# Seven row blocks normalised on GpSimd, none on ScalarE, in a newly ordered attention-plus-gated-MLP kernel on one Trainium2 core

## The chip, the cores and the metric

The kernel runs on one core of one Trainium2 chip. The core has five instruction queues that run on their own and wait for each other through semaphores: TensorE (PE, matrix multiplies), VectorE (DVE), ScalarE (ACT), GpSimd (POOL) and SyncE (SP), which here issues nearly all DMAs. The metric is the device time of one execution in microseconds (us): the median of three runs before the change is 272.52 us (272.19 to 273.63).

## The reference

One pre-norm transformer layer over 2048 rows of width 640 in bf16, with a linear attention of 32 heads of 20 and a gated MLP of width 1536:

```python
def _A_ref(x, wqkv, w_phi, wo):
    ...
    pq = jnp.einsum("bhsd,hdf->bhsf", q, w_phi)
    pk = jnp.einsum("bhsd,hdf->bhsf", k, w_phi)
    phi_q = jnp.concatenate([_softmax(pq, axis=-1), _softmax(-pq, axis=-1)], axis=-1)
    phi_k = jnp.concatenate([_softmax(pk, axis=-1), _softmax(-pk, axis=-1)], axis=-1)
    kv = jnp.einsum("bhsf,bhsd->bhfd", phi_k, v)
    z  = jnp.einsum("bhsf->bhf", phi_k)
    ...
    o = num / den
    return (lambda x, *d: x.transpose(*d))(o, 0, 2, 1, 3).reshape(B, S, D) @ wo
def _B_ref(x, w_gate, w_up, w_down):
    g = jnp.einsum("bsd,df->bsf", x, w_gate)
    u = jnp.einsum("bsd,df->bsf", x, w_up)
    h = g * u
    return jnp.einsum("bsf,fd->bsd", h, w_down)
h = x + _A_ref(_layernorm(x, axis=-1), A_wqkv, A_w_phi, A_wo)
h2 = h + _B_ref(_layernorm(h, axis=-1), B_w_gate, B_w_up, B_w_down)
```

## The kernel before

The 2048 rows are 16 tiles of 128 (t = 0 to 15). Each piece of work is an *operation* with a name, made by `G.op`; its engine, emitter, inputs and outputs stand beside the name. The names that the text uses, with the tile's number behind them:

- `x`: load of one or two x tiles. `w5`: load of the feature weights, 25 KB. `wk`, `wv`: 128 rows of the K and V weights. `wqt`: transposing load of a piece of the Q weights. `wo`, `wg`, `wu`, `wd`: the later weights.
- `L1s`, `L1a`: the row statistics of the first norm on VectorE (lines 406 to 409). `L1l`, `L1e`: logarithm and exponential on ScalarE, which give one over the standard deviation in `rs` (L414, L417).
- `L1n`: a 128x1 operation that puts minus mean times `rs` into `nb` (L421), the *shift* of the ScalarE form below.
- `xn`: the normalised tile. VectorE computes (x minus mean) times `rs` (L431); ScalarE computes x times `rs` plus `nb` (L429). In the kernel before, 13 tiles are made on VectorE and three (7, 10 and 11) on ScalarE.
- `xt`: the transposed tile in `xnT`; tiles 0 and 1 by TensorE (`xte` takes the result out of PSUM), all others by a DMA transpose that SP issues (L449).
- `WT`, `WTe`: transposes of the K weights on TensorE, and their evacuation. `Ph0` to `Ph2`: the block-diagonal feature weights, which need `w5` (L358). `F1`, `F0`: the feature weights folded into the K and the Q weights on TensorE (L389), with evacuations `Fe`. F1 needs all `Ph` and a `WTe`, F0 needs all five `wqt`.
- `K`, `V`, `Q`: projections of a tile on TensorE, ten matmuls each (L460). `Kx`: two exponentials on ScalarE (L472); `Ks`: the sums on VectorE (L476); `Kr`, `Ke`: their reciprocal on ScalarE (L479, L481); `Kn`: the division, 128x1280 on GpSimd (L496). `KV`: kv and z, accumulated on TensorE over all 16 tiles (L504); `KVe` takes them out after KV15.
- `Qx`, `Qs`, `Qr`, `Qb`, `Qe`, `Qn`: the same for Q (L529 to L548, `Qb` and `Qn` on GpSimd); `qT`: DMA transpose of the result (L553). `N`: numerator and denominator (L566); `dd`, `rd`, `o`: the division; `oT`: its DMA transpose (L597); `O`: output projection (L603); `h`, `hc`, `hT`: residual, centring, DMA transpose.
- `U`: gate and up projections (L646) in five blocks of rows, `D`: down projection (L665), `y` and `w`: the last addition and the store.

Where an operation stands is written out by hand in a table of text, `PLAN`: name, place, the number of an alternative engine (0 or left out is the first), and the PSUM banks or buffers that it takes. `arrange` sorts by place and hands each engine its operations; every engine then works strictly in that order, and SP issues its DMAs strictly in that order. An operation at the head of a queue that waits holds up all that stand behind it. The few lines that decide this:

```python
k, a, o.slots = PLAN.get(name, (key, 0, ()))
o.eng, o.occ, o.lat = o.alts[a]
...
for o in sorted(G.ops, key=lambda o: (o.key, o.i)):
    order[o.eng].append(o)
```

Of the kernel before, what the change touches and what calls it, by code (L numbers as in the profile page):

```python
# [57 lines left out]
F1_0:75::4 xn1:76::3 F1_2:77::0 L1e3:78 Fe1_0:79:1 WTe3:80 L1n3:81 WT4:82::2 xt1:83::3 xn3:84::0 Fe1_2:85:1 F1_3:86::6 xte1:87:1 K0_0:88::4 xt3:89 Fe1_3:90
K0_1:91 WTe4:92:1 K0_2:93 L1s2:94 V0_0:95::0 F1_4:96::2 wqt0:97 V1_0:98::6 Fe1_4:99:1 V1_1:100 L1s4:101 K0_3:102 V1_2:103 K1_0:104::2 L1a2:105 L1s5:106
wqt3:107 L1l2:108 K1_1:109 K0_4:110 L1e2:111 K1_2:112 L1n2:113:1 L1a4:114 K1_3:115 L1a5:116 xn2:117::2 L1l4:118 K1_4:119 V0_1:120 L1e4:121 Kx0_0:122::0  # L60
xt2:123 V0_2:124 L1n5:125:1 L1n4:126 xn5:127::3 V0_3:128 Kx0_1:129 V0_4:130 L1s6:131 V1_3:132 Kx1_0:133::1 V1_4:134 x10:135 V3:136::4 L1s7:137 Kx1_1:138
xt5:139 Ve1:140::0 L1a6:141 xn4:142::0 K3:143::2 Ks0:144::0 Ve3:145::1 x8:146 Ve0:147::2 xt4:148 K2:149::4 L1a7:150 Ks1:151::1 L1l6:152 Kx3_0:153::2 wqt4:154
Kx3_1:155 V2:156::0 L1s11:157 L1e6:158 Kx2_0:159::3 L1n6:160 wqt1:161 L1n7:162 Kr0:163 Ks3:164::2 Kx2_1:165 K5:166::2 Ke0:167 Kr1:168 wqt2:169 Ve2:170::3
Kn0:171 xn6:172::3 V5:173::4 xn7:174:1:2 L1s9:175 xt6:176 Kx5_0:177::4 Ks2:178::3 V4:179::6 Ke1:180 Kx5_1:181 Kn1:182 xt7:183 Ve5:184::4 L1s8:185 F0_4:186::2
Kr2:187 Kr3:188 F0_3:189::0 Ke2:190 x14:191 Fe0_4:192:1 K4:193::4 Fe0_3:194 x12:195 L1a9:196 L1a8:197 Kn2:198 Ve4:199::5 Ks5:200::1 wo2:201 KV0:202::2,3
L1l8:203 L1e8:204 F0_2:205::0 Kx4_0:206::0 V6:207::6 L1n9:208:1 L1n8:209:1 xn9:210::0 Kx4_1:211 L1s10:212 rqz:213 xt9:214 Fe0_2:215 KV1:216 Ke3:217 L1a11:218
F0_0:219::4 Kr5:220 xn8:221::1 Kn3:222 K7:223::0 Fe0_0:224 Ks4:225::3 xt8:226 Ve6:227::0 F0_1:228::4 Kx7_0:229::1 L1a10:230 wg0:231 KV2:232 L1s14:233
K6:234::6 Kr4:235 wu1:236 mk1:237 Kx7_1:238 L1s15:239 Ke4:240 Fe0_1:241 Kn4:242 L1a14:243 KV3:244 Ks7:245::2 L1l10:246 K9:247::0 Kx6_0:248::3 Kx6_1:249
L1s13:250 L1e10:251 Ke5:252 Q0_0:253::4 Kx9_0:254::2 Q0_1:255 Kn5:256 L1n10:257:1 Q1_0:258::6 L1a13:259 L1s12:260 Kx9_1:261 Q1_1:262 Q0_2:263 Q1_2:264
xn10:265:1:0 L1a15:266 Q0_3:267 L1a12:268 Ks6:269::3 Q1_3:270 Q1_4:271 L1l12:272 xt10:273 Kr7:274 Q0_4:275 L1e12:276 Ke7:277 K8:278::0 L1n11:279 Qx1_0:280::3  # L70
Kn7:281 Ks9:282::1 Qx1_1:283 wo0:284 KV4:285 Kr6:286 wg2:287 Qx0_0:288::1 KV5:289 Qs1:290 Q3:291::6 Qx0_1:292 L1n13:293 L1n15:294 Ke6:295 Kx8_0:296::4
L1n12:297 Kn6:298 Qs0:299 V7:300::4 Kx8_1:301 Qr1:302::2 Qx3_0:303::0 xn13:304::1 Q5:305::0 Qx3_1:306 Ve7:307:1:5 xt13:308 Qb1:309 Qr0:310::0 Kr9:311
L1n14:312 xn15:313::2 Qb0:314 Ke9:315 mk2:316 KV6:317 Kn9:318 Qx5_0:319::2 Ks8:320::3 K10:321::6 wg1:322 xn11:323:1:3 Qs3:324 Qx5_1:325 Q2:326::4 xt11:327
Kr8:328 Qe1:329 smz:330 Kx10_0:331::3 Qn1:332 xn12:333::0 xt15:334 Q9:335::0 Ke8:336 Kx10_1:337 xn14:338::1 Qx2_0:339::4 Qs5:340 Kn8:341 xt12:342 KV7:343
Qx2_1:344 V8:345::6 Qr3:346::1 Qx9_0:347::5 Qs2:348 wg3:349 Qe0:350 K13:351::4 wu2:352 Qb3:353 Ve8:354::5 Qn0:355 Ks10:356::0 Qe3:357 Qx9_1:358 K11:359::6
Kx13_0:360::1 Qn3:361 Kx13_1:362 V9:363::0 Kx11_0:364::0 qT3:365::0 Qr2:366::3 Qr5:367::0 Kr10:368 Qb2:369 Qb5:370 KV8:371 Ke10:372 Kx11_1:373 Ve9:374:1:1
Kn10:375 K12:376::4 xt14:377 Ks13:378::3 V10:379::0 qT1:380::4 Kx12_0:381::4 Ks11:382::1 Kx12_1:383 K15:384::6 Qe5:385 Kr13:386 wd2:387 Ve10:388::6 Qn5:389
Ks12:390::0 qT0:391::1 Ke13:392 Kr11:393 Ke11:394 KV9:395 Qe2:396 Kn13:397 Q4:398::0 Kx15_0:399::2 Qs9:400 qT5:401::2 Kx15_1:402 K14:403::4 Qx4_0:404::0
Ks15:405::2 Kn11:406 Qx4_1:407 KV10:408 Qr9:409::1 V14:410::6 Kx14_0:411::3 Kr15:412 Ke15:413 wu0:414 Q10:415::0 Qb9:416 Ve14:417:1:7 Qn2:418 Qe9:419
Kx14_1:420 Qs4:421 V13:422::6 Kn15:423 Qx10_0:424::1 qT2:425::3 Kr12:426 Ks14:427::1 Ke12:428 Qr4:429::0 V12:430::4 Qx10_1:431 wu3:432 Ve13:433::3 Kn12:434  # L80
Kr14:435 V11:436::0 Ve12:437:1:6 Qs10:438 Q13:439::6 Ve11:440::0 Ke14:441 Kn14:442 V15:443::0 Qx13_0:444::3 Qx13_1:445 KV11:446 Ve15:447::5 Qs13:448 KV12:449
KV13:450 Qn9:451 Qr10:452::2 KV14:453 KV15:454 Q6:455::4 KVe0:456 Qb4:457 qT9:458::5 Qe4:459 Qn4:460 KVe1:461 Qx6_0:462::4 N0:463::2 N2:464::6 dd0:465::1
qT4:466::1 Qx6_1:467 Q7:468::0 rd0:469 dd2:470::0 o0:471::0 Qr13:472::3 rl2:473 Qb13:474 rd2:475 Qb10:476 o2:477::1 N1:478::4 Qx7_0:479::2 Q11:480::2
oT0:481::0 dd1:482::0 Qx7_1:483 rd1:484 o1:485::2 N9:486::6 oT2:487::1 Qx11_0:488::5 N3:489::0 dd9:490::0 Q8:491::4 rd9:492 Qx11_1:493 dd3:494::3 rd3:495
oT1:496::2 Qe13:497 o3:498::0 Qn13:499 O0:500::2 Qx8_0:501::0 oT3:502::3 o9:503::1 Qx8_1:504 O2:505::0 Qe10:506 h0:507 oT9:508::0 Qs7:509 hc0:510::3 N5:511::2
O1:512::4 qT13:513::2 h2:514 Qr7:515::3 Qb7:516 Qn10:517 O3:518::6 h1:519 hT0:520 hc1:521::2 N4:522::0 h3:523 Q14:524::4 L2q1:525 hT1:526 dd5:527::2
dd4:528::0 rl5:529 rd4:530 hc2:531::1 o4:532::1 O9:533::6 rd5:534 qT10:535::0 Qx14_0:536::3 o5:537::0 Qx14_1:538 Q12:539::0 h9:540 oT4:541::0 Qs14:542
U0_1_0:543::2 wd3:544 U0_0_0:545::6 g0_1:546::1 N13:547::4 oT5:548::3 U0_2_0:549::7 Qx12_0:550::1 dd13:551::1 Qs8:552 U0_0_1:553::2 g0_0:554::3 g0_2:555::0
hT2:556 U0_2_1:557::3 Qx12_1:558 U0_5_0:559::7 u0_0:560::0 Qr14:561::2 L2q2:562 rd13:563 Qb14:564 U0_1_1:565::6 wd1:566 hc3:567:1:0 O4:568::0 Qr8:569::0
u0_1:570 o13:571::2 u0_2:572 U0_3_0:573::6 Qs6:574 U0_4_0:575::2 g0_3:576::0 L2q0:577 O5:578::4 h4:579 Qe7:580 g0_5:581::1 Qn7:582 g0_4:583::2 U0_11_0:584::3  # L90
Qe14:585 hc4:586:1:3 h5:587 N10:588::0 U0_3_1:589::7 L2v1:590 qT7:591::2 Qn14:592 L2q5:593 U0_6_0:594::6 u0_3:595 U0_9_1:596::5 dd10:597::2 rd10:598 Qb8:599
hT3:600 U0_5_1:601::4 o10:602::1 L2v0:603 U0_4_1:604::7 U0_7_0:605::2 oT13:606::3 u0_4:607 Q15:608::0 L2v5:609:1 u0_5:610 g0_7:611::0 hc9:612:1:2 g0_6:613::3
hc5:614::1 hT4:615 U0_7_1:616::6 Qr6:617::3 Qx15_0:618::2 U0_6_1:619::7 hT5:620 Qx15_1:621 U0_8_0:622::2 u0_6:623 g0_11:624::2 U0_10_1:625::4 u0_7:626
# [813 lines left out]
```

## Time and profile before

| | us |
|---|---|
| median of three runs | 272.52 |
| the profiled execution | 272.19 |
| its span on the core | 270.5 |
| TensorE busy in the span | 264.4 |
| VectorE, ScalarE busy | 157.0, 123.4 |

The profiled execution is the fastest of the three; 1.7 us of its time lie outside the span. A matmul's record lasts longer than the matmul holds the array, so a busy TensorE is not one at its peak, and a wait costs its idle time and the overlap of two records as well. The granted TensorE clock is 1.00 but for the last few microseconds.

### The profile page before, as it was taken

How to read it: one execution, taken by the hardware profiler on the slowest of the kernel's cores; microseconds unless marked ns; L12 is line 12 of the kernel's file. 1: busy time of each engine (PE TensorE's matmuls, PEld its weight loads, DVE VectorE, ACT ScalarE, POOL GpSimd, SP SyncE). 2: the span in 40 equal slices, each digit the busy share in tenths (PEclk: the TensorE clock that was granted, in tenths of full speed). 3: DMA queues.
4: the chain of work that ended last, by engine and by line, in shares of the span. 5: the costliest groups of instructions: out<-in, count | busy, mean ns of one | idle time of the engine just before them, and what ended most of it. 6: DMA issues, size and time to landing. Idle time of an engine off the chain costs nothing.

```text
span 270.5 us, 5196 instructions
## 1 busy us (share of the span) xinstructions
PE 264.4 (98%) x2103; PEld 177.5 (66%) x2103; DVE 157.0 (58%) x296; ACT 123.4 (46%) x317; POOL 70.7 (26%) x86
## 2 busy tenths in 40 slices
...
GB/s 202 265 155 182 203 194 168 198 206 204 175 141 112 165 191 127 100 106 133 67 27 153 81 2 72 27 24 73 27 46 102 25 0 2 0 0 1 51 73 73
DMA packets 71752, 28.09 MB, mean 104 GB/s; under 512 B 59056, under 2 KB 71728, under 8 KB 71728
## 3 DMA queue, kind: packets, MB, share of 16 engines
...
q10 hardware_dynamic: 288, 0.33, 0.4%
q14 instruction: 8, 0.07, 0.1%
...
## 4 chain that ended last, share of the span: by engine, by line
PE 83%; DMA 6%; DVE 4%; ACT 3%; SPq 2%; POOL 1%; issue 1%; DVEq 0%
PE ps L646 39%; PE ps L665 19%; PE ps L460 14%; PE ps L603 8%; SPq L263 2%; DMA scratch<-ph 2%; DMA xnT<-xn 2%; DMA x_all<-in_A_x_dram 2%; PE ps L566 2%; ACT ek L472 1%; DVE SR L476 1%; POOL ek L496 1%; PE ps L504 1%; ACT ev L229 1%; DVE st L407 1%
## 5 line engine op out<-in xcount | busy, mean ns | idle before, releaser
L646 PE MATMUL ps<-xnT,Wgu 128*128 128x512 bf16 (+1 forms) x600 | 108.1, 336 | 0.2 <-issue 0.2
L646 PEld LDWEIGHTS ps<-xnT,Wgu 128*128 128x128 bf16 x600 | 58.0, 98 | 42.7 <-DVE ev L654 0.8
L651 ACT ACTIVATE gt<-ps 128x512 bf16<-128x512 f32 (+1 forms) x60 | 29.3, 511 | 97.1 <-PE ps L646 86.1
L460 PE MATMUL ps<-Wp,xnT 128*128 128x320 bf16 (+1 forms) x480 | 68.6, 299 | 0.2 <-DMA xnT<-xn 0.2
L654 DVE TENSOR_TENSOR ev<-ps,gt 128x512 bf16<-128x512 f32 (+1 forms) x60 | 34.0, 579 | 57.7 <-PE ps L646 43.5
L460 PEld LDWEIGHTS ps<-Wp,xnT 128*128 128x128 bf16 x480 | 45.5, 97 | 17.6 <-DMA xnT<-xn 0.3
L665 PE MATMUL ps<-Wd,ev 128*128 128x320 bf16 (+2 forms) x396 | 53.8, 295 | 0.0
L665 PEld LDWEIGHTS ps<-Wd,ev 128*128 128x128 bf16 x396 | 38.2, 98 | 15.4
L496 POOL TENSOR_TENSOR ek<-ek,SR 128x1280 bf16<-128x1280 bf16 x16 | 37.5, 2360 | 3.8 <-ACT SR L481 3.7
L548 POOL TENSOR_TENSOR ph<-ph,RQ 128x660 bf16<-128x660 bf16 x16 | 20.9, 1311 | 28.6 <-ACT RQ L544 28.5
L677 DVE SCALAR_TENSOR_TENSOR Wp<-ps,rs,x_all 128x640 bf16<-128x640 f32 (+3 forms) x18 | 14.3, 806 | 22.7 <-PE ps L665 20.2
L534 DVE TENSOR_REDUCE S<-ph 128x66 f32<-128x1320 bf16 x16 | 24.1, 1520 | 2.1 <-ACT ph L531 2.0
L603 PE MATMUL ps<-Wo,Wp 128*128 128x320 bf16 x160 | 23.5, 299 | 0.0
L529 ACT ACTIVATE ph<-ps 128x600 bf16<-128x600 f32 x32 | 21.4, 683 | 4.0 <-PE ps L460 2.6
L476 DVE TENSOR_REDUCE SR<-ek 128x64 f32<-128x1280 bf16 x16 | 23.2, 1464 | 0.0
L472 ACT ACTIVATE ek<-ps 128x640 bf16<-128x640 f32 x32 | 21.4, 708 | 1.7 <-PE ps L460 1.3
L609 DVE SCALAR_TENSOR_TENSOR x_all<-ps,x_all 128x640 bf16<-128x640 f32 x16 | 13.1, 821 | 12.4 <-PE ps L603 12.4
L603 PEld LDWEIGHTS ps<-Wo,Wp 128*128 128x128 bf16 x160 | 15.6, 98 | 6.6 <-issue 0.2
L624 POOL TENSOR_SCALAR ln<-mv 128x1 f32<-128x1 f32 x6 | 1.2, 192 | 62.3 <-ACT ek L620 62.0
L593 DVE TENSOR_TENSOR o<-ps,sm 128x660 bf16<-128x660 f32 x16 | 13.4, 843 | 4.3 <-ACT sm L586 3.3
L620 ACT ACTIVATE ek<-x_all,mv 128x640 bf16<-128x640 bf16 x16 | 13.2, 823 | 1.2 <-DVE x_all L609 1.2
L618 ACT ACTIVATE xn<-x_all,mv 128x640 bf16<-128x640 bf16 x10 | 8.1, 822 | 6.1 <-DVE x_all L609 6.1
...
## 6 DMA issues: line engine op xcount, KB each, us to landing
out_dram<-Wp SPq DMA_DIRECT2D x15, 160.0 KB, 1.9
...
Wp<-in_A_wqkv_dram SPq DMA_DIRECT2D x5, 160.0 KB, 4.6
ev<-in_A_wqkv_dram SPq DMA_DIRECT2D x4, 160.0 KB, 3.8
x_all<-in_A_x_dram SPq DMA_DIRECT2D x3, 160.0 KB, 3.7
```

Source lines behind the costliest of these rows:

```text
L460: ins = e.matmul(pb(b, hb)[:, 0:n1 - n0], lhsT=T["xnT"][:, NC - 1 - c, P * t:P * (t + 1)], rhs=T["Wp"][:, POS[kind], c, n0:n1], start=(c = ...
L472: G.op("act", "%sx%d_%d" % (nm, t, s), lambda e, s=s, b=b, ek=ek: e.activation(out=T["ek"][:, ek.slots[0], 0:2 * D].rearrange("p (b h s f) ...
L476: G.op("dve", "%ss%d" % (nm, t), lambda e, ek=ek, sr=sr: e.tensor_reduce(out=T["SR"][:, sr.slots[0], 0, :], in_=T["ek"][:, ek.slots[0], 0: ...
L496: G.op("pool", "Kn%d" % t, lambda e, eng, ek=ek, sr=sr: e.tensor_tensor(out=T["ek"][:, ek.slots[0], 0:2 * D].rearrange("p (h f) -> p h f", ...
L529: e.activation(out=v[:, 0:10].rearrange("p (b g) j f -> p b g j f", b=2), in_=pp(b, 0, 300).rearrange("p b (g j f) -> p b g j f", j=3, f=D ...
L534: G.op("dve", "Qs%d" % t, lambda e, t=t, ph=ph: e.tensor_reduce(out=T["S"][:, t, 0:66].rearrange("p (g k) -> p g k", k=6), in_=pv(ph).rear ...
L548: return e.tensor_tensor(out=v, in0=v, in1=T["RQ"][:, rq.slots[0], 1, 0:33].rearrange("p (g j) -> p g j", j=3).unsqueeze(3).to_broadcast([ ...
L603: ins = e.matmul(pb(b, hb)[:, 0:320], lhsT=T["oT"][:, oT.slots[0], c, :], rhs=T["Wo"][:, c, 320 * hb:320 * (hb + 1)], start=(c == 0), stop ...
L646: ins = e.matmul(pb(b)[:, 0:n], lhsT=T["Wgu"][:, gu, c, P * ft:P * (ft + 1)], rhs=T["xnT"][:, NC - 1 - c, o0:o0 + n], start=(c == 0), stop ...
L651: G.op("act", "g%d_%d" % (bi, ft), lambda e, pg=pg, gt=gt, n=n: e.activation(out=T["gt"][:, gt.slots[0], 0:n], in_=pb(pg)[:, 0:n], func=AF ...
L654: o_ = G.op("dve", "u%d_%d" % (bi, ft), lambda e, pu=pu, gt=gt, hh=hh, ft=ft, n=n: e.tensor_tensor(out=T["hh"][:, hh.slots[0], ft, 0:n], i ...
L665: ins = e.matmul(pb(b, hb)[:, 0:w], lhsT=T["hh"][:, hh.slots[0], ft, P * tt:P * (tt + 1)], rhs=T["Wd"][:, ft, c0 + w * hb:c0 + w * (hb + 1 ...
```

## The change

Three edits. The 14 shift operations `L1n` and their buffer `nb` are gone, with the ScalarE form of `xn`. In its place `xn` has GpSimd as its second engine, with the formula that VectorE uses. And the table `PLAN` is written anew: in it tiles 2, 3, 5, 6, 10, 11 and 13 are normalised on GpSimd and the other nine on VectorE; the order on all engines, the order of the DMAs and the banks differ, while all other operations are the same. `Ph1` and `Ph2` move from GpSimd to VectorE, and `w5` from the head of SP's queue to its fourth place.

```diff
-zero:0 x0:1:1 id0:2 w5:3:1 eps:4 warm0:5 gl0:6 x3:7:1 wk0:8 warm1:9 warm2:10 gla:11 wk1:12 warm3:13 id1:14 warm4:15 warm5:16 glb:17 x1:18 warm6:19 ekz:20
+x1:0:1 zero:1 id0:2 x0:3 gl0:4 warm0:5 x3:6:1 wk0:7 warm1:8 id1:9 warm2:10 wk1:11 warm3:12 gla:13 warm4:14 glb:15 warm5:16 w5:17:1 eps:18 Sz:19 warm6:20
...
-    nb_b = [Buf("nb%d" % t) for t in range(NT)]
...
-        for t in tl:
-            if t > 1:
-                G.op("pool", "L1n%d" % t, lambda e, eng, t=t: e.tensor_scalar(
-                    out=T["nb"][:, t:t + 1], in0=T["mv"][:, t, 0:1], scalar1=T["rs"][:, t:t + 1], scalar2=-1.0, op0=ALU.mult,
-                    op1=ALU.mult), 0.2, LP, [rs_b[t], mv_b[t]], [nb_b[t]], 10 * t - 25, alts=[("dve", 0.07, LD)])
...
-            if eng == "act":
-                return e.activation(out=rev(xb), in_=T["x"][:, t, :].rearrange("p (c n) -> p c n", c=NC), func=AF.Identity,
-                                    scale=T["rs"][:, t:t + 1], bias=T["nb"][:, t:t + 1])
             return e.tensor_scalar(out=rev(xb), in0=T["x"][:, t, :].rearrange("p (c n) -> p c n", c=NC),
                                    scalar1=T["mv"][:, t, 0:1], scalar2=T["rs"][:, t:t + 1], op0=ALU.subtract, op1=ALU.mult)
-        G.op("dve", "xn%d" % t, xn, 0.5, LD, [x_b[t], mv_b[t], rs_b[t], nb_b[t]], [xb], 10 * t - 22,
-             alts=[] if t < 2 else [("act", act_c(640, True), LA)])
+        G.op("dve", "xn%d" % t, xn, 0.5, LD, [x_b[t], mv_b[t], rs_b[t]], [xb], 10 * t - 22,
+             alts=[] if t < 2 else [("pool", 0.95, LP)])
```

Three places show how the order moves. The changed kernel has fewer lines, so its line numbers are 2 to 10 lower. First, the head of SP's queue before (`w` is the feature weights of `w5`, `ev` the `wk`, `Wp` the `wv`):

```order
L263 DMA w<-in_A_w_phi_dram 128x5x20
L263 DMA x_all<-in_A_x_dram 128x640
L263 DMA ev<-in_A_wqkv_dram 128x640
L263 DMA x_all<-in_A_x_dram 128x640
L263 DMA ev<-in_A_wqkv_dram 128x640 x2
```

and now:

```order
L261 DMA x_all<-in_A_x_dram 128x640 x2
L261 DMA ev<-in_A_wqkv_dram 128x640
L261 DMA w<-in_A_w_phi_dram 128x5x20
L261 DMA ev<-in_A_wqkv_dram 128x640 x3
L261 DMA Wp<-in_A_wqkv_dram 128x640
```

The feature weights went behind two x tiles and one piece of the K weights; ScalarE's queue, which held x0 and wk0, now holds x1 and wk0.

Second, TensorE where the Q weights are folded. `ps<-Wp,xnT` are projections, `ps<-Phi,scratch` folds (six matmuls each), `ps<-ev,ek` the KV products. Before:

```order
L460 MATMUL ps<-Wp,xnT 128x320 x102
L389 MATMUL ps<-Phi,scratch 128x140 x2
L389 MATMUL ps<-Phi,scratch 128x80 x2
L389 MATMUL ps<-Phi,scratch 128x140 x4
L389 MATMUL ps<-Phi,scratch 128x80 x2
L389 MATMUL ps<-Phi,scratch 128x140 x2
L460 MATMUL ps<-Wp,xnT 128x320 x10
L504 MATMUL ps<-ev,ek 128x63 x10
```

and now:

```order
L450 MATMUL ps<-Wp,xnT 128x320 x106
L494 MATMUL ps<-ev,ek 128x63 x10
L494 MATMUL ps<-ev,ek 128x42
L494 MATMUL ps<-ev,ek 128x63 x10
L494 MATMUL ps<-ev,ek 128x42
L387 MATMUL ps<-Phi,scratch 128x140 x2
L387 MATMUL ps<-Phi,scratch 128x80 x2
L387 MATMUL ps<-Phi,scratch 128x140 x4
```

KV0 and KV1 now stand ahead of the first fold F0_4; before, the folds came first.

Third, GpSimd's queue from the end of its setup (`nb` is the shift, `ek` the division `Kn`, `Phi` is `Ph`). Before:

```order
L421 TENSOR_SCALAR nb<-mv,rs 128x1 x4
L496 TENSOR_TENSOR ek<-ek,SR 128x1280 x3
L331 MEMSET RQ 128x4
L496 TENSOR_TENSOR ek<-ek,SR 128x1280
L336 AFFINE_SELECT mask<-mask 128x33
L496 TENSOR_TENSOR ek<-ek,SR 128x1280 x2
L421 TENSOR_SCALAR nb<-mv,rs 128x1
L496 TENSOR_TENSOR ek<-ek,SR 128x1280
L421 TENSOR_SCALAR nb<-mv,rs 128x1 x3
```

and now:

```order
L421 TENSOR_SCALAR xn<-x_all,mv,rs 128x5x128 x2
L324 MEMSET ph 128x6x40
L325 MEMSET ph 128x66x8
L486 TENSOR_TENSOR ek<-ek,SR 128x1280 x2
L421 TENSOR_SCALAR xn<-x_all,mv,rs 128x5x128
L486 TENSOR_TENSOR ek<-ek,SR 128x1280 x2
L421 TENSOR_SCALAR xn<-x_all,mv,rs 128x5x128 x2
L486 TENSOR_TENSOR ek<-ek,SR 128x1280 x2
L421 TENSOR_SCALAR xn<-x_all,mv,rs 128x5x128
```

Six of the seven rows stand ahead of the fifth division, Kn4 (tile 3's is ahead of what is shown, right behind `Ph0`), and one, tile 13's, behind Kn5. From Kn4 to the last Kn the other work is the same but for the shifts, `mk1` and one `Qb`.

More of the change, by code (lines that the diff above doesn't have):

```diff
@@ L58 @@
[L58 to L93, printed above, removed]
@@ L122 @@
[L122 to L123 removed]
+x1:0:1 zero:1 id0:2 x0:3 gl0:4 warm0:5 x3:6:1 wk0:7 warm1:8 id1:9 warm2:10 wk1:11 warm3:12 gla:13 warm4:14 glb:15 warm5:16 w5:17:1 eps:18 Sz:19 warm6:20
+mk0:21 warm7:22 wk2:23:1 warm8:24::5 warm9:25 wk3:26 warm10:27 warm11:28 wk4:29:1 warm12:30 L1s1:31 warm13:32 wv0:33:1 warm14:34 warm15:35 L1s0:36 x2:37
@@ new lines @@
+WT1:38::1 wv3:39 warm16:40 L1a1:41 L1a0:42 wv1:43 L1s3:44 L1l0:45 L1l1:46 x4:47 L1e0:48 WTe1:49:1 xn0:50::0 WT0:51::4 wv2:52:1 warm17:53 warm18:54 Ph2:55:1
+Ph0:56 WTe0:57 warm19:58 Ph1:59:1 xt0:60::1 x6:61 L1a3:62 WT2:63::3 L1l3:64 xte0:65:1 wv4:66:1 F1_1:67::6 L1e1:68 WTe2:69 xn1:70::3 WT3:71::5 F1_0:72::0
+Fe1_1:73 WTe3:74 WT4:75::2 xt1:76::3 Fe1_0:77 L1e3:78 WTe4:79 F1_2:80::4 xn3:81:1:0 F1_3:82::6 xte1:83:1 Fe1_2:84:1 K0_0:85::0 L1s2:86 K0_1:87 ekz:88 Fe1_3:89
+xt3:90 F1_4:91::2 rqz:92 va1:93 K1_0:94::4 Fe1_4:95:1 L1a2:96 K1_1:97 L1s4:98 K0_2:99 L1l2:100 K0_3:101 x10:102 V0_0:103::2 L1s5:104 L1e2:105 K0_4:106
@@ new lines @@
+xn6:171:1:0 Kx5_0:172::4 Ks2:173::2 Kx5_1:174 xt6:175 V4:176::2 L1a11:177 xn7:178::2 Kr2:179 Ke2:180 Ve5:181::4 L1a8:182 L1a10:183 xt7:184 Kn2:185 Ks3:186::1
+KV0:187::6,7 Ve4:188::5 KV1:189 F0_4:190::0 L1l10:191 x12:192 F0_2:193::4 L1s9:194 Kr3:195 K4:196::2 L1e10:197 x14:198 Fe0_2:199 L1a9:200 Fe0_4:201:1 L1l8:202
+Ke3:203 L1e8:204 KV2:205 Kn3:206 xn9:207::1 Kx4_0:208::0 F0_3:209::4 Ks5:210::2 V6:211::0 xt9:212 Fe0_3:213 Kx4_1:214 F0_0:215::4 xn8:216::0 Ve6:217::0
+K7:218::2 xn10:219:1:3 Ks4:220::0 xt8:221 Fe0_0:222 xn11:223:1:2 Kr5:224 K6:225::0 L1s14:226 Kx7_0:227::2 xt10:228 Kx7_1:229 L1s15:230 F0_1:231::4 wu3:232
```

93 lines of the change are left out of this document (59 added, 34 removed).

## The prediction

> **What bounds the kernel now.** I read the busy shares first, then TensorE's own waits, then its timeline at those waits, then the queues that feed it.
>
> ```profile
> PE 264.4 (98%) x2103; PEld 177.5 (66%) x2103; DVE 157.0 (58%) x296; ACT 123.4 (46%) x317; POOL 70.7 (26%) x86
> PE ps L389 <- ACT SR L481: 0.5, 1, 0.5
> PE ps L440 <- DVE xn L431: 0.4, 1, 0.4
> PE ps L566 <- DMA scratch<-ph: 0.3, 1, 0.3
> PE ps L460 <- DMA xnT<-xn: 0.2, 1, 0.2
> ```
>
> TensorE bounds it, and the change takes no matmul away. So it can gain only waits. From the first useful matmul on these four (each row: us in total, times, longest) come to 1.4 us, and a fifth of 0.16 stands in the chain of waits below. The loss is a little larger, since a wait also breaks the overlap of two records:
>
> ```profile
> 40.86 4.10 PE ps L460 x30
> 109.89 0.16 issue
> L460 PE MATMUL ps<-Wp,xnT 128*128 128x320 bf16 x320 | 46.1, 299 | 0.2 <-DMA xnT<-xn 0.2
> ```
>
> Thirty projections' matmuls pass in 4.10 us, 0.137 each, while one record lasts 0.299: a wait costs its idle time and some 0.16 more. Five waits: 1.4 + 0.16 + 5 x 0.16 = 2.4 us; no order gains much more, beside what it gains before the first useful matmul. A worse order, though, can lose any amount.
>
> ```profile
> 5.42 0.45 PE L370 MATMUL ps<-ident,ev 128*128 128x128 bf16 x5 [0.79 <-DMA ev<-in_A_wqkv_dram]
> 9.81 1.25 PE L460 MATMUL ps<-Wp,xnT 128*128 128x320 bf16 x8
> 25.83 0.80 PE L389 MATMUL ps<-Phi,scratch 128*128 128x140 bf16 x12 [0.55 <-ACT SR L481]
> 34.56 1.66 PE L460 MATMUL ps<-Wp,xnT 128*128 128x320 bf16 x11 [0.19 <-DMA xnT<-xn]
> 72.34 1.85 PE L504 MATMUL ps<-ev,ek 128*128 128x63 bf16 x55
> 79.66 0.85 PE L566 MATMUL ps<-KVm,scratch 128*128 128x63 bf16 x22 [0.33 <-DMA scratch<-ph]
> ```
>
> These are the places, followed now one by one: WT1 at 5.42, the first projection at 9.81, F0_4 at 25.83, K9 at 34.56, the block KV11 to KV15 from 72.34, N9 at 79.66, and U1's start at 110.05 behind the 0.16 of the chain.
>
> **The start, -0.2 us.** Ahead of K0_0 both orders put the same five transposes, two x transposes and four folds on TensorE, and the same twelve fillers; what differs is when their inputs land.
>
> ```profile
> 0.80 0.46 SPq L263 DMA_DIRECT2D w<-in_A_w_phi_dram  x1
> w<-in_A_w_phi_dram SPq DMA_DIRECT2D x1, 25.0 KB, 2.6
> Wp<-in_A_wqkv_dram SPq DMA_DIRECT2D x5, 160.0 KB, 4.6
> L358 POOL TENSOR_TENSOR Phi<-w,GL 128x280 bf16<-128x280 bf16 x2 | 1.3, 656 | 0.1
> L406 DVE BATCH_NORM_STATS2 st<-x_all 128x6 f32<-128x320 bf16 x16 | 7.6, 474 | 3.0 <-DMA x_all<-in_A_x_dram 2.9
> ```
>
> w5 now issues fourth, about 1.4 us later, behind three 160 KB loads: between 0.80 + 1.4 + 2.6 = 4.8 and, at the larger loads' 4.6, 6.8; I take 5.7. Ph0 (0.66) then ends at 6.4 on GpSimd; Ph1 and Ph2 go to VectorE behind xn0, at some 7.1. Statistics begin when x1 lands, near 3.3, cost two times 0.9 for two tiles, and with logarithm, exponential and the row itself put xt0 near 6.6 and F1_1 near 7.2. The five transposes and four folds are then through at about 9.6 against 9.81. Ends: -0.4, and +0.6 if w5 lands at 6.8.
>
> **The folds, -0.5 us, and K9, -0.35 us.** F0_4 needs the five transposed Q weights:
>
> ```profile
> 21.18 2.59 SPq L287 DMA_TRANSPOSE scratch<-in_A_wqkv_dram  x2
> 26.45 1.10 SPq L263 DMA_DIRECT2D x_all<-in_A_x_dram  x2
> 27.60 0.47 SPq L263 DMA_DIRECT2D Wo<-in_A_wo_dram  x1
> 29.50 3.12 SPq L449 DMA_TRANSPOSE xnT<-xn  x2
> DMA to landing us min/median/max: 3.1/3.8/4.5
> DMA to landing us min/median/max: 2.6/3.2/5.0
> 44.96 0.34 PE ps L504 x11
> ```
>
> The last of two issued from 21.18 leaves at 22.5 and lands 3.1 later, at 25.6: that is F0_4's wait, though the row names ScalarE. Now KV0 and KV1 (0.34 each) stand ahead of the folds and fill 0.68 of 0.71; they need Kn1, which I put at 22.1, since Kn0 starts earlier. Adding up SP's new queue, its last Q weight issues near 21.8 and lands between 24.9 and 26.3 (3.1 to 4.5). I take -0.5; ends -0.7 and +0.3. K9 waited for tile 9's transpose, issued at 29.50 behind two 320 KB x loads and 480 KB of Wo, at the maximum of 5.0. Wo now comes later and tile 9 goes out near 28: even at 5.0 it lands at 33.0, and K9 is due at 33.5. I take -0.35 (ends -0.35 and 0).
>
> **GpSimd's pace, +0.2 us.** No row of the trace is a GpSimd `xn`. The bounds and the cover:
>
> ```profile
> L327 POOL MEMSET ph<- 128x528 bf16 x1 | 0.5, 538 | 0.0
> L548 POOL TENSOR_TENSOR ph<-ph,RQ 128x660 bf16<-128x660 bf16 x16 | 20.9, 1311 | 28.6 <-ACT RQ L544 28.5
> L496 POOL TENSOR_TENSOR ek<-ek,SR 128x1280 bf16<-128x1280 bf16 x16 | 37.5, 2360 | 3.8 <-ACT SR L481 3.7
> L421 POOL TENSOR_SCALAR nb<-mv,rs 128x1 f32<-128x1 f32 x9 | 2.3, 269 | 13.9 <-ACT rs L417 13.9
> L431 DVE TENSOR_SCALAR xn<-x_all,mv,rs 128x640 bf16<-128x640 bf16 x13 | 7.6, 588 | 0.0
> L429 ACT ACTIVATE xn<-x_all,nb,rs 128x640 bf16<-128x640 bf16 x3 | 2.8, 927 | 0.0
> 6.00:20.00 14.00, 13.53 (x134) 10.27 (x134) 13.67 (x34) 11.45 (x25) 0.60 (x3) 1.00 0.90 217
> 33.73:73.10 39.37, 39.18 (x376) 28.93 (x374) 33.42 (x37) 34.65 (x100) 37.09 (x31) 1.00 0.82 197
> ```
>
> It lies between a fill that reads nothing (0.54) and a product of two tensors of nearly this size (1.31); with one tensor read I take the middle, 0.95. The page "GPSIMD Engine Reference" of the Trainium skill (section 3.1) gives at best 1.8 cycles an element at 1.2 GHz, an estimate of 0.96 for 640 elements, and the sum would be the same.
>
> ScalarE loses 3 x 0.93 = 2.8 us, VectorE four rows of 0.59 and five shifts: no gain by itself, since TensorE is busy 39.18 of 39.37 us there. GpSimd gains 7 x 0.95 and loses nine shifts of 0.27. Six of the seven rows fall before Kn4, where GpSimd had room (0.60 busy of 14.00 us). The price is in what follows: from Kn4 to the last division GpSimd was busy 37.09 of 39.37 us. Now that stretch holds 37.09 - 5 x 0.24 (shifts, as they follow each other) + 0.95 (tile 13) + 0.31 + 0.21 (a mask operation, a `Qb`) = 37.4. Kn4 can start when K6's exponentials and Kr4, Ke4 are through:
>
> ```profile
> 19.11 1.19 ACT ek L472 x2
> 20.98 0.14 ACT SR L479
> ```
>
> With TensorE 1.05 ahead (0.2 + 0.5 + 0.35), K9 starts at 33.5 and K6, which F0_1 and KV3 now follow, ends at 32.85; two exponentials of 0.6 and two small ones of 0.14 put Kn4 at 34.5, later than the 33.73 of before. 34.5 + 37.4 = 71.9, and following the queue by hand I find 0.8 us in which it waits for Qr0, Ke8 and Qe3: Kn15 ends at 72.7. TensorE reaches KV15 (55 matmuls from 72.34, the last eleven from 73.70) at 73.70 - 1.05 = 72.65. Both arrive together; I add 0.2. Ends: 0, and +1.6, if GpSimd waits the old 2.28 us there. Behind KV15 stand KVe0 and KVe1, and all of N for them.
>
> **N9 -0.45, O0 +0.2, U1 -0.4 us.** N9 waited for a DMA transpose issued at 74.39, right after the last `Qn`; now Q8 (1.37) and N3 precede it, which covers 0.49. O0's turn comes about when its own transpose lands:
>
> ```profile
> 74.39 3.14 SPq L553 DMA_TRANSPOSE scratch<-ph  x2
> Wp<-o SPq DMA_TRANSPOSE x16, 2.7
> ```
>
> By my addition it issues near 76.6, behind the transpose of Q4, and needs 2.7, or 3.8 (the median of the weights' transposes above) beside another: O0, due at 80.1, waits 0 to 0.6. U1's two small waits of 0.16 go, since by the new order O4 ends some 5 us before U1, time enough for h4, its centring and a transpose of 2.6 to 3.2, as the x transposes above (ends -0.5, +0.5).
>
> **The sum**: -0.2 - 0.5 - 0.35 + 0.2 - 0.45 + 0.2 - 0.4 = -1.5, from the profiled execution's 272.19: 270.7. The median of the runs shown lies 0.3 above it, so 271.0.
>
> **The rivals.** (1) *GpSimd keeps its old pace*: it waits 2.28 us between Kn4 and Kn15, and KV15 waits 1.6 instead of 0.2. For it: 28.5 us of waits for ScalarE in `Qn`'s row; against it: at most 2.28 of those lie in this stretch, and the new queue asks for its inputs later. Time: 271.0 + 1.4 = 272.4, no change. (2) *The rows cost more than a product*, as much as a 1280-wide one, 2.36. Then xn3, xn2 and xn5, each at the head of GpSimd's queue, are late, and so is SP, whose transposes of x and of the Q weights stand behind them: F0_4 waits about 1.0, and tile 13's row adds 1.4 to Kn15. 271.0 + 2.4 = 273.4, slower; it decides from about 1.8 us a row. Against it: one operand is one number per row. (3) *w5 late*, at 8 us or beyond: F1_1 and all behind it start 1.5 to 2 us later, nothing makes it up, and the other gains stand: 273.0. For it: 4.6 us for a load of 160 KB issued among many. (4) *A port shared by VectorE and GpSimd*:
>
> ```profile
> 22.22 0.60 DVE L431 TENSOR_SCALAR xn<-x_all,mv,rs 128x640 bf16<-128x640 bf16 x1
> 21.94 6.99 POOL L496 TENSOR_TENSOR ek<-ek,SR 128x1280 bf16<-128x1280 bf16 x3 [0.96 <-ACT SR L481]
> ```
>
> VectorE's row at 22.22 ran inside GpSimd's Kn0 in 0.60, no longer than elsewhere (0.588), so neither blocked the other. If it did at the start, xte1 would wait up to 0.95 for xn3 and K1_0 some 0.4: 271.4. The Trainium skill, "SBUF — State Buffer" (Who interferes with whom), has a VectorE copy or scalar operation in a two-port mode and a GpSimd operation lock each other out for the whole instruction; by that rule the row inside Kn0 would have waited, and it did not, so the trace does not bear it out for this shape.
>
> **How the numbers follow.** The sum 0.45, rival 1 0.27, rival 2 0.13, rival 3 0.10, rival 4 0.05. A change under 0.5% (1.36 us) can't be told from none. The sum lies just beyond that bound: its own range, 270.2 to 271.9, is faster for 0.37 and the same for 0.08. Rival 1 splits 0.02, 0.20 and 0.05; rivals 2 and 3 are slower but for 0.04; rival 4 is faster for 0.02, the same for 0.03. So 0.41 faster, 0.35 same, 0.24 slower. The range goes from 269.7 (all waits gone: 272.5 less 2.4, and 0.4 at the start) to 273.7, which takes in rival 2.
>
> **What would show it.** No wait of TensorE for `scratch` at the first fold and none for `xnT` at K9; K0_0 at 9.6; a GpSimd row of 0.95 at L421; Kn15 ending within 0.3 of KV15's turn; N9 without a wait. Wrong would be: a TensorE wait for `ek` before KV15 over 1 us, a row of 1.8 or more, Ph0 starting after 6.8, or a new wait over 1 us at a DMA transpose behind 76 us.

## The result, and the profile after

The changed kernel takes 275.22 us (median; 274.71 to 276.14) against 272.44 for the kernel before on the same chip: a ratio of 1.0095, with an interval of 1.0072 to 1.0118. It is slower by 2.8 us, and beyond the upper end of the range (273.7). The profiled execution took 275.25 us, its span 273.5 (before 272.19 and 270.5).

First the busy shares of the page, and from the groups with forms kept apart the two large kinds of work on GpSimd (group | busy us, mean ns of one | idle before and releaser):

```profile
PE 265.4 (97%) x2103; PEld 177.1 (65%) x2103; DVE 157.5 (58%) x293; ACT 120.1 (44%) x312; POOL 83.8 (31%) x80
```

```profile
L421 POOL TENSOR_SCALAR xn<-x_all,mv,rs 128x640 bf16<-128x640 bf16 x7 | 17.5, 2503 | 2.7 <-ACT rs L415 2.7
L486 POOL TENSOR_TENSOR ek<-ek,SR 128x1280 bf16<-128x1280 bf16 x16 | 37.5, 2359 | 2.2 <-ACT SR L471 2.1
```

One normalised row block costs GpSimd 2.50 us, not 0.95: more than a division over twice as many elements. GpSimd's busy time rose from 70.7 to 83.8 us. Then what TensorE waited for (us in total, times, longest):

```profile
PE ps L387 <- DMA scratch<-in_A_wqkv_dram: 1.3, 1, 1.3
PE ps L450 <- ACT ph L521: 1.0, 1, 1.0
PE ps L430 <- DVE xn L421: 0.8, 1, 0.8
PE ps L450 <- DMA xnT<-xn: 0.6, 2, 0.3
PE ps L593 <- DMA Wp<-o: 0.2, 1, 0.2
```

And TensorE's timeline at the places of the prediction (start, us, work, in brackets the idle time and its releaser):

```profile
7.25 0.44 PE L430 MATMUL ps<-ident,xn 128*128 128x128 bf16 x5 [0.80 <-DVE xn L421]
10.13 0.72 PE L450 MATMUL ps<-Wp,xnT 128*128 128x320 bf16 x4
21.92 2.89 PE L450 MATMUL ps<-Wp,xnT 128*128 128x320 bf16 x20 [0.33 <-DMA xnT<-xn]
25.07 1.53 PE L450 MATMUL ps<-Wp,xnT 128*128 128x320 bf16 x10 [0.26 <-DMA xnT<-xn]
26.44 0.84 PE L494 MATMUL ps<-ev,ek 128*128 128x63 bf16 x22
28.54 0.80 PE L387 MATMUL ps<-Phi,scratch 128*128 128x140 bf16 x12 [1.26 <-DMA scratch<-in_A_wqkv_dram]
53.41 1.53 PE L450 MATMUL ps<-Wp,xnT 128*128 128x320 bf16 x10 [1.00 <-ACT ph L521]
```

These are xt0's transposes, K0_0, K5, V4, KV0 with KV1, F0_4 and K13. The loss at a wait is read from the starts: KV0 and KV1 begin at 26.44 and need 0.68 at the rate of before, so F0_4 was due at 27.12 and started at 28.54: 1.42 us. In the same way K5 lost 0.50, V4 0.43 and K13 1.15. K9 and N9 no longer wait, and U1's start lost nothing.

**Where the first loss comes from** stands on two queues side by side. GpSimd's first three rows, xn3, xn2 and xn5:

```profile
9.69 2.50 POOL L421 TENSOR_SCALAR xn<-x_all,mv,rs 128x640 bf16<-128x640 bf16 x1 [2.70 <-ACT rs L415]
13.26 4.99 POOL L421 TENSOR_SCALAR xn<-x_all,mv,rs 128x640 bf16<-128x640 bf16 x2
```

and SP's queue:

```profile
12.21 1.29 SPq L439 DMA_TRANSPOSE xnT<-xn  x1
15.79 1.23 SPq L439 DMA_TRANSPOSE xnT<-xn  x1
18.27 1.20 SPq L439 DMA_TRANSPOSE xnT<-xn  x1
23.47 2.71 SPq L285 DMA_TRANSPOSE scratch<-in_A_wqkv_dram  x2
```

xn3 ends at 12.19 and its transpose leaves at 12.21; xn2 at 15.76 and 15.79; xn5 at 18.25 and 18.27. SP works strictly in order, so all behind these waits too: the last two pieces of the Q weights are issued from 23.47 instead of 21.18 (the prediction's row), the very last at 24.78, and it lands at 28.45. K5 waits for tile 5's transpose, V4 for tile 4's, and F0_4 for the last Q weight.

**The second loss** is followed back in the chain of waits (start, us, what; the short pieces between are left out):

```profile
32.84 4.97 POOL xn L421 x2
37.81 4.64 POOL ek L486 x2
42.45 2.48 POOL xn L421
...
44.96 2.56 DMA xnT<-xn
...
47.55 0.04 DVE xn L421
...
48.07 1.52 DVE S L524
...
50.90 1.53 DVE S L524
...
52.70 0.56 ACT ph L519
...
53.41 0.72 PE ps L450 x4
```

xn10 and xn11 (4.97 us) stand ahead of Kn4 and Kn5, and xn13 behind those. xn13 is ready at 44.93 and its transpose lands at 47.52. Only then is its buffer free for xn15, which VectorE had reached before and waited for; the sums behind it are late, so ScalarE's reciprocals and Q2's exponentials behind them, and K13 needs the bank that these exponentials empty.

### The profile page after: what moved, and what is told of

Same layout as the page of the kernel before. It is cut to its first block, busy times and chain, and to the rows that moved or that the text cites. A ratio compares the mean times of both kernels' runs of the same rounds, so it can differ in the third digit from the quotient of the medians.

```text
span 273.5 us, 5183 instructions
## 1 busy us (share of the span) xinstructions
PE 265.4 (97%) x2103; PEld 177.1 (65%) x2103; DVE 157.5 (58%) x293; ACT 120.1 (44%) x312; POOL 83.8 (31%) x80
## 4 chain that ended last, share of the span: by engine, by line
PE 82%; POOL 5%; DMA 5%; DVE 4%; ACT 1%; issue 1%; SPq 1%; DVEq 0%; ACTq 0%
PE ps L636 38%; PE ps L655 19%; PE ps L450 13%; PE ps L593 8%; POOL xn L421 3%; POOL ek L486 3%; PE ps L556 1%; DMA scratch<-in_A_wqkv_dram 1%; PE ps L494 1%; DMA x_all<-in_A_x_dram 1%; DVE S L524 1%; DMA Wp<-o 1%; DMA xnT<-xn 1%; PE ps L387 1%; DVE st L404 1%
## 5 line engine op out<-in xcount | busy, mean ns | idle before, releaser
L641 ACT ACTIVATE gt<-ps 128x512 bf16<-128x512 f32 (+1 forms) x60 | 29.3, 511 | 89.2 <-PE ps L636 70.7
L644 DVE TENSOR_TENSOR ev<-ps,gt 128x512 bf16<-128x512 f32 (+1 forms) x60 | 33.4, 579 | 46.5 <-PE ps L636 32.8
L421 POOL TENSOR_SCALAR xn<-x_all,mv,rs 128x640 bf16<-128x640 bf16 x7 | 17.5, 2503 | 2.7 <-ACT rs L415 2.7
```

The source lines that it names most:

```text
L421: return e.tensor_scalar(out=rev(xb), in0=T["x"][:, t, :].rearrange("p (c n) -> p c n", c=NC), scalar1=T["mv"][:, t, 0:1], scalar2=T["rs"] ...
L641: G.op("act", "g%d_%d" % (bi, ft), lambda e, pg=pg, gt=gt, n=n: e.activation(out=T["gt"][:, gt.slots[0], 0:n], in_=pb(pg)[:, 0:n], func=AF ...
L644: o_ = G.op("dve", "u%d_%d" % (bi, ft), lambda e, pu=pu, gt=gt, hh=hh, ft=ft, n=n: e.tensor_tensor(out=T["hh"][:, hh.slots[0], ft, 0:n], i ...
```

## The experiments

Two theories stood against each other: the *price*, by which 2.50 us a row makes the whole loss, and the *order*, by which the new order had lost what it should have gained even at a low price. A third question was why the start gained nothing. In the entries of `PLAN` shown below, the number behind the place names the engine: 1 is GpSimd for an `xn`, none is VectorE. Each ratio is against the kernel before on the same chip.

**All seven rows back on VectorE, in the new order.**

```diff
-xn3:81:1:0  xn2:107:1:1  xn5:126:1:3  xn6:171:1:0  xn10:219:1:3  xn11:223:1:2  xn13:275:1:1
+xn3:81::0   xn2:107::1   xn5:126::3   xn6:171::0   xn10:219::3   xn11:223::2   xn13:275::1
```

> The changed kernel, its order word for word, but the seven rows on VectorE in the same places of the order. Theory A (the GpSimd row's price of 2.5 us holds up SP's queue and the rows behind it): TensorE's waits at K5 (0.50), V4 (0.43), F0_4 (1.42) and K13 (1.15) go, 3.5 us, and VectorE's 7 x 0.52 = 3.6 us more give back some: 271.5 to 272.5. Theory B (the new order of the loads makes the waits, whatever engine makes the rows): the waits at F0_4 and K5 stay, 274 or more.

272.91 us, ratio 1.0033 (1.0012 to 1.0054). Nearly two thirds of the loss are gone, with the waits of K5 and V4; F0_4 lost 0.15. K13 still lost 0.64, and the time lies above the 271.5 to 272.5 of theory A. So the rows on GpSimd make most of the loss, but the new order with the rows on VectorE is no gain either.

**Only the first four (tiles 2, 3, 5, 6) back on VectorE.** The edit is the first four entries of the one above.

> As the changed kernel, but only tiles 2, 3, 5 and 6 on VectorE; 10, 11 and 13 stay on GpSimd. Theory A: K5, V4 and F0_4 lose their waits (2.3 us), K13 keeps its 1.15: 272.5 to 273.2. Theory B: 274 or more, F0_4 still waits over 1 us.

273.11 us, 1.0039 (1.0018 to 1.0059). K5 and V4 do not wait, F0_4 lost 0.15; in TensorE's timeline K13 remains, with tile 13 still on GpSimd:

```profile
51.52 1.53 PE L454 MATMUL ps<-Wp,xnT 128*128 128x320 bf16 x10 [1.45 <-ACT ph L525]
```

**Only tile 13 back on VectorE.**

```diff
-xn13:275:1:1
+xn13:275::1
```

> As the changed kernel, but only tile 13 on VectorE. Theory A: K13's 1.15 us goes, the earlier waits stay: 273.9 to 274.5. Rival (K13 waits because TensorE and ScalarE are late for other reasons): no change, 275.

274.27 us, 1.0081 (1.0056 to 1.0106). Now K13 stands in its timeline without an idle time:

```profile
51.80 1.53 PE L454 MATMUL ps<-Wp,xnT 128*128 128x320 bf16 x10
```

while K5 and V4 lost 0.66 and 1.03, and F0_4 0.27. The two losses are two: each goes with its own rows. The second is worth less in the time than in the trace (0.9 us less at K13, 0.4 us in the median, with intervals that overlap).

**What makes a row cost 2.50 us.** The seven rows in seven forms, in one execution; six of them leave out parts of the normalisation or write the blocks in plain order. A `tensor_scalar` (*scalar operation* below) combines each element with a constant or with one number per row, a `tensor_tensor` (*product*) with an element of a second tensor.

Each form in words:

```diff
+            if t == 2: tensor_scalar, two operations, numbers per row, plain block order
+            if t == 5: tensor_scalar, one operation, number per row
+            if t == 6: tensor_scalar, two operations, constants
+            if t == 10: tensor_scalar, one operation, constant
+            if t == 11: tensor_tensor, x times rs broadcast over the row
+            if t == 13: tensor_copy
```

> The output is not the reference's: six of the seven GpSimd rows are replaced by other forms, each writing its 640 elements in plain order, to price them: tile 2 subtract and multiply by two per-row numbers; 5 one multiply by a per-row number; 6 subtract and multiply by two constants; 10 one multiply by a constant; 11 a product of two tensors, the second a per-row number broadcast; 13 a copy. Tile 3 keeps the full form with reversed blocks. If the reversed blocks make the 2.5 us: tile 2 near 1. If the per-row numbers do: tile 2 at 2.5, tiles 6 and 10 near 1. If it is two operations an element: tiles 2 and 6 at 2.5, tiles 5 and 10 at 1.3. If it is the two-port sharing with VectorE: all forms vary from tile to tile with what VectorE does.

The groups with forms apart, the first being tile 3 in the form of the change; the lines differ since each form has its own:

```profile
L438 POOL TENSOR_SCALAR xn<-x_all,mv,rs 128x640 bf16<-128x640 bf16 x1 | 2.5, 2507 | 2.7 <-ACT rs L419 2.7
L427 POOL TENSOR_SCALAR xn<-x_all,mv,rs 128x640 bf16<-128x640 bf16 x1 | 2.5, 2503 | 0.0
L431 POOL TENSOR_SCALAR xn<-x_all 128x640 bf16<-128x640 bf16 x1 | 2.4, 2360 | 0.1
L429 POOL TENSOR_SCALAR xn<-x_all,rs 128x640 bf16<-128x640 bf16 x1 | 1.9, 1892 | 0.0
L433 POOL TENSOR_SCALAR xn<-x_all 128x640 bf16<-128x640 bf16 x1 | 1.8, 1826 | 0.1
L435 POOL TENSOR_TENSOR xn<-x_all,rs 128x640 bf16<-128x640 bf16 x1 | 1.3, 1254 | 0.1
L437 POOL COPY xn<-x_all 128x640 bf16<-128x640 bf16 x1 | 0.7, 722 | 0.0
```

The reversed blocks cost nothing (2507 against 2503). Two numbers per row instead of two constants cost 0.14. A copy takes 0.72; one scalar operation takes 1.1 more, and the second operation 0.53 more. A product, which takes a second operand for every element, is cheaper than one scalar operation. The price is that of the operation's form; why the form costs so much no run shows.

**The new order with cheap rows.** The rows on GpSimd as a copy (0.72 us; it leaves out the normalisation), and as a product (1.25 us; it leaves out the mean):

```diff
+            if eng == "pool":
+                return e.tensor_copy(out=T["xn"][:, xb.slots[0], :], in_=T["x"][:, t, :])
```

> The output is not the reference's: in the changed kernel the seven GpSimd rows are plain copies of the x tile (0.72 us), near the 0.95 of the prediction's sum and of the order's own plan; all else is the change word for word. Theory A (the price of the row is all that the prediction had wrong): 271.0 as its sum, no wait at F0_4 and K9. Theory C (the new order is also limited by GpSimd's pace between Kn4 and Kn15, whatever the rows cost): 272 to 273, with Kn4 after 34.5 and KV15 waiting or K13 waiting in its place.

```diff
+            if eng == "pool":
+                return e.tensor_tensor(out=T["xn"][:, xb.slots[0], :], in0=T["x"][:, t, :],
+                                       in1=T["rs"][:, t:t + 1].to_broadcast([P, D]), op=ALU.mult)
```

> The output is not the reference's: the seven GpSimd rows are one product of the x tile with the broadcast rs, without the mean (1.25 us). Theory A: between the copy's time and the change's, on a line through the price: with 0.72 us at 271.0 and 2.50 at 275.2, some 272.2; the waits of TensorE at K5, V4 and F0_4 shorter by half or more. Theory C: close to the copy's time, since six of seven rows lie beside the pace.

272.44 us, 0.9989 (0.9967 to 1.0011), with the copy; 272.55 us, 1.0004 (0.998 to 1.0027), with the product. So the price makes 1.0095 - 0.9989 = 1.06%, some 2.9 us (2.0 to 3.8, the intervals taken together): the whole loss against the kernel before. Between 0.72 and 1.25 us a row the time is the same. But these prices lie on either side of the assumed 0.95, and neither kernel is shown to be faster than before (0.3 us less with the copy, 0.1 more with the product, each within its interval): the gain of 1.5 us was not there. Theory C has the time of both, but not its reason: in neither profile does KV15 or K13 wait. The product's profiled execution (271.72 us, below its median) shows where the gain went, in TensorE's timeline:

```profile
9.86 0.72 PE L457 MATMUL ps<-Wp,xnT 128*128 128x320 bf16 x4
...
25.14 0.84 PE L501 MATMUL ps<-ev,ek 128*128 128x63 bf16 x22
26.70 0.80 PE L391 MATMUL ps<-Phi,scratch 128*128 128x140 bf16 x12 [0.73 <-issue]
...
75.24 0.84 PE L563 MATMUL ps<-KVm,scratch 128*128 128x63 bf16 x22
75.93 1.53 PE L457 MATMUL ps<-Wp,xnT 128*128 128x300 bf16 x10
77.30 0.84 PE L563 MATMUL ps<-KVm,scratch 128*128 128x63 bf16 x22
78.24 2.92 PE L457 MATMUL ps<-Wp,xnT 128*128 128x300 bf16 x20
```

K0_0 starts at 9.86, not 9.6. F0_4 was due at 25.14 + 0.68 = 25.82 and starts at 26.70: 0.88 lost, where the prediction left 0.2 (with the copy 0.79). And Q11 comes 0.25 late: 22 matmuls of N take 0.69 from 75.24 to 75.93, but 0.94 from 77.30 to 78.24.

**The old order without shifts and ScalarE rows**: the before's `PLAN` with all 14 `L1n` taken out and tiles 7, 10 and 11 on VectorE.

> The order of the kernel before, without the shift operations, and the three rows that ScalarE made on VectorE. ScalarE loses 2.8 us, VectorE gains 1.6 and loses five shifts, GpSimd loses nine shifts (2.1 us). Theory A or C (the loss of the change lies in the GpSimd rows and the new order): no worse than before, 271.5 to 272.4. Rival (the ScalarE form was needed, VectorE is full): over 273.

272.12 us, 0.9998 (0.9979 to 1.0017). Taking that work off ScalarE and GpSimd shows no gain by itself.

**The old order with its waits swapped away**: K4 ahead of the folds, one piece of Wo later, N9 behind more work.

```diff
-K4:193::4   wo2:201   N9:486::6   dd3:494::3   rd3:495
+K4:185.5::4 wo2:226.5 N9:489.1::6 dd3:489.2::3 rd3:489.4
```

> The kernel before with three steps moved by hand: K4 ahead of F0_4, the larger Wo load behind tile 8's transpose, N3 ahead of N9 with its two VectorE steps. Each takes up one wait that the prediction named: 0.5, 0.35 and 0.34 us. If those waits bind by themselves: 271.0 to 271.5. If GpSimd's pace to Kn15 binds behind them: the first two are given back at KV15 and only the third counts, 271.8 to 272.2.

272.40 us, 0.9993 (0.9979 to 1.0007). F0_4, K9 and N9 no longer waited, but KV0 lost 0.85 where F0_4 had lost 0.71, and U's blocks 0.57 where they had lost 0.47. Three waits of the prediction were taken away together, and the time stayed: their 1.55 us came back further on (0.85 at KV0, 0.46 at three projections around it, 0.15 at O0, 0.1 in U). The largest of these is of the swap's own making. In `PLAN` KV0 takes PSUM banks 2 and 3, which F0_4 has filled; VectorE takes this fold out from 26.87 to 27.69, and KV0 starts at 27.84. Before, K4 stood between the two and covered that time.

**More matmuls ahead of the first transpose, old order** (six *fillers* more before WT1; a filler is a matmul of zeros whose result nobody uses), because TensorE passes its first matmuls at half the rate (last section).

> The kernel before with six more filler matmuls ahead of WT1, which close the idle time of TensorE there. Theory D (where the first K weights land late, TensorE falls back to half its speed, 0.213 instead of 0.109 us for 256 columns, for some 4 us, and that makes the spread of the runs): median 272.0 to 272.3 and fewer runs over 273. Rival (the spread has nothing to do with the start): the same spread, median 272.4 to 272.6, since a late WT1 costs the fillers' time.

272.60 us, 1.0013 (0.9999 to 1.0028). The gap ahead of WT1 was filled, and in the profile the half rate lasted until 7.1 us all the same, so it doesn't need the gap (theory D). The time is the rival's.

**A better version of the new order**: only tile 10 on GpSimd, and Q2's exponentials earlier in ScalarE's queue; then with wk1 ahead of the second x load; then with six fillers more.

```diff
-xn11:223:1:2  Qx2_0:320::4    Qx2_1:327    (and tiles 2, 3, 5, 6, 13 as in the first experiment)
+xn11:223::2   Qx2_0:316.5::4  Qx2_1:319.5
```

> The new order with only tile 10 on GpSimd, in the gap ahead of Kn4, the other six on VectorE, and the two exponentials of Q2 on ScalarE ahead of Kr8 and of Ke9, so that K13's banks come free early. Theory A with C: no wait over 0.3 at K5, V4 and F0_4, none over 0.3 at K13, GpSimd ends Kn15 as TensorE arrives: 271.8 to 272.3, at or just under the kernel before. If K13's wait only hid that GpSimd is late: the wait moves to KV15, 272.8.

> e10 with wk1's load ahead of x3's on SP. Theory D: WT1 starts near 4.8 instead of 5.3 to 5.9, TensorE does not fall back, but the next wait, for xt0, stays near 7: 0.1 to 0.4 us less than e10 and less spread. Rival (only x1 and xn0 limit the start): equal to e10 within 0.2.

> e11 with six more fillers between WT0 and xt0. Theory D: TensorE keeps its speed up to the first projection, least spread of all, 271.3 to 271.9 and under the kernel before. Rival: equal to e11.

273.12 us, 1.0033 (1.002 to 1.0046); 273.11, 1.0031 (1.0013 to 1.0048); 273.84, 1.0055 (1.0038 to 1.0073), in the profile of which F0_4 lost 1.43. All three lie above what theories A and D expected. In the first of the three K13's wait is gone, and TensorE's waits show another one in its place, KV15 behind GpSimd's divisions:

```profile
PE ps L498 <- POOL ek L490: 0.5, 1, 0.5
```

With wk1 issued earlier WT1 still started at 5.29. No version of the new order that computes the layer came below the kernel before.

**Three rows on GpSimd in the old order** (tiles 7, 10 and 11, which ScalarE had made; the shifts taken out; nothing else moved). This tells whether seven rows cost what they do because of the new order or in spite of it.

> The changed code with the order of the kernel before: tiles 7, 10 and 11, which ScalarE made, on GpSimd, and no shifts. Tile 7 stands behind the first division's place in the queue, tiles 10 and 11 inside GpSimd's full stretch from Kn4 to Kn14, where it had 2.3 us of idle time and loses 1.2 us of shifts. Theory A: 2 x 2.5 us there less 1.2 and part of 2.3: KV15 waits 1.5 to 3 us, 273.8 to 275.5. Rival (rows on GpSimd hurt only through the new order): 272.0 to 272.6.

277.69 us, 1.0193 (1.0168 to 1.0217): three rows cost more there than seven in the new order, and more than theory A expected. TensorE's waits:

```profile
PE ps L454 <- ACT ph L525: 2.3, 2, 1.7
PE ps L454 <- DMA xnT<-xn: 2.1, 4, 1.1
PE ps L498 <- POOL ek L490: 0.3, 1, 0.3
```

and the rows in GpSimd's timeline:

```profile
23.88 2.50 POOL L425 TENSOR_SCALAR xn<-x_all,mv,rs 128x640 bf16<-128x640 bf16 x1
...
39.28 2.51 POOL L425 TENSOR_SCALAR xn<-x_all,mv,rs 128x640 bf16<-128x640 bf16 x1
...
49.38 2.51 POOL L425 TENSOR_SCALAR xn<-x_all,mv,rs 128x640 bf16<-128x640 bf16 x1
```

Two of the three lie inside the stretch from Kn4 on, where GpSimd had 2.3 us to spare, and 1.2 more without the shifts, and they need 5.0. The new order puts only one there; it is the better order for rows on GpSimd. But KV15 did not wait, as theory A had it: the losses come before it, the largest 1.25 us at K9, whose transposed tile lands late, and 1.88 at a projection at 73.80, which waits for exponentials of Q on ScalarE.

**The swaps and the missing shifts together**, in the old order.

> The old order with the three hand moves, no shifts, tiles 7, 10 and 11 on VectorE. If ScalarE's 2.8 us and GpSimd's 2.1 us were what gave the moves back: 271.2 to 271.9, under the kernel before. If the waits only move on (PSUM banks of the folds, the pace to Kn15): 272.0 to 272.5, the same.

272.36 us, 1.002 (0.9999 to 1.004). No gain; KV0 and U wait as with the swaps alone.

## Why the prediction was wrong, point by point

The step that failed first is the price of a row: "with one tensor read I take the middle, 0.95", between a fill of 0.54 and a product of 1.31. It measured 2.50. Both were real rows, but the product was no upper bound. A scalar operation on GpSimd costs more than a product of the same size (1.83 to 2.50 against 1.25), so the argument that one tensor read less makes it cheaper was false. The Trainium skill goes the way of that argument: "GPSIMD Engine Reference", section 4.1, has operations with one input at about line rate on GpSimd, those with two slower. Here the copy (0.72) bears that out and the scalar operations do not; the measurement decides. At the 1.2 GHz that this page of the Trainium skill gives (section 3.1) the row took an estimated 2503 x 1.2 / 640 = 4.7 cycles an element, against the best case of 1.8 that the prediction cited.

A second part failed beside it: of the gain of 1.5 us, the runs with rows of 0.72 and 1.25 us show 0.3 and -0.1, neither clear of noise. In the product's profile three terms fell short: F0_4 by 0.7 us, since the last Q weight left later than the addition of SP's queue had it; the start by 0.26; and Q11 by 0.25, a wait that the prediction didn't have.

Against the sum's 270.7, the profiled 275.25 is 4.55 more. The parts, as losses of TensorE read from its starts:

| step | predicted | measured |
|---|---|---|
| the start (K0_0) | 9.6 | 10.13, 0.5 more |
| K5 and V4 | no wait | 0.93 more |
| F0_4 | 0.2 left | 1.42, 1.2 more |
| K9, N9, U1 | waits gone | gone |
| K13 | no wait | 1.15 more |
| KV15 (GpSimd's pace) | 0.2 | 0.13 |
| Q11 | no wait | 0.26 more |
| O0 and O1 | 0.2 | 0.45, 0.25 more |

The rows of the table come to 4.2 of the 4.55; the rest is spread over many starts.

- **The start.** x1 landed at 3.98, not near 3.3, and xt0 started at 7.25, not 6.6; WT1 started at 5.28 against 5.42. The feature weights landed at 6.26 instead of 5.7, inside the ends given; Ph0 started at 6.34, so rival 3 did not occur. In the profiles with this start of the queues K0_0 started between 9.63 and 11.2, in those of the old order with its own twelve fillers between 9.59 and 9.96: the scatter from execution to execution is larger than the term of 0.2, and nothing shows a gain.
- **The folds.** KV0 and KV1 stand there and fill 0.68 us as said. But SP's new queue issues the last Q weight later than "near 21.8": by the trace at 24.78, at 22.96 with the product, and at 22.63 with tiles 2, 3, 5 and 6 on VectorE, where no GpSimd row stands ahead of it. So this term is wrong in two parts: some 0.8 us of the lateness is of the addition of SP's queue, the larger rest of the price.
- **K9.** The wait is gone, but in part by luck: with the product tile 9's transpose went out at 29.33, not near 28, but landed after 3.5 us instead of 5.0.
- **GpSimd's pace.** The mechanism held and the size nearly too: from Kn4 to the end of Kn15 both kernels with cheap rows took some 37.8 us (predicted 37.4, and 0.8 of waiting). With rows of 2.50 Kn4 starts at 37.77 instead of 34.5, and the stretch shows GpSimd full (columns: window, its length, busy us and number of PE, PEld, DVE, ACT, POOL, clock, DMA share, GB/s):

```profile
37.77:76.61 38.84, 37.84 (x371) 27.91 (x369) 33.12 (x34) 31.82 (x95) 38.70 (x30) 1.00 0.80 191
```

GpSimd is busy 38.70 of 38.84 us. Kn15 ends at 76.61 and KV15 starts at 76.66: TensorE loses almost nothing here, but only since it had been made late before.

- **Rival 2** had the mechanism, and "decides from about 1.8 us a row" is not contradicted: 1.25 is no change, 2.50 is. Its 273.4 came out too low, since it put tile 13's price at Kn15 (1.4) and the wait at F0_4 at about 1.0. The trace has 1.42 there, waits at K5 and V4 before it, and tile 13's price at K13, through the buffer that VectorE waits for. What it was held down by, one number per row as the operand, was measured to cost 0.14 for two.
- **Rival 4**, the shared port: the rows took 2.498 to 2.513 us in every run and at every place, whatever VectorE did beside them, and VectorE's rows 0.55 to 0.61 with and without them. Nothing speaks for it. In which mode VectorE's rows run no trace here shows, so the row inside Kn0 tells of this shape and doesn't test the rule that the prediction names.
- **Rival 1** needs GpSimd to wait; it was full, and with the product KV15 did not wait either.

Settled by runs: the price, its dependence on the form of the operation, both places of the loss, and that the gain of 1.5 us was not there at a low price. Open: why the form costs so much, and how much the start's scatter hides in the medians. Why the order with all rows on VectorE (1.0033) stays above the one with copies on GpSimd (0.9989) was not tested. The profiles fit a VectorE that is late: with all rows on it TensorE loses 0.42 and 0.38 where VectorE has yet to take a result out of PSUM (at 12.12 and 37.41), and 0.64 at K13; with the copies it loses nothing at these three.
